# Queries by (head, 32 tokens), one sketch weight for all heads, early denominators for batch 0, and loads that wait for the weights

## The chip, the cores and the metric

The kernel runs on one core of a Trainium2 chip. A core has the engines PE (TensorE, matrix products; PEld is its loading of weights), DVE (VectorE), ACT (ScalarE), POOL (GpSimd) and SP (SyncE, which here only issues DMAs). They run beside each other and wait for each other through semaphores; 16 DMA engines move data. The metric is the device time of one launch in microseconds, the median of several runs; fewer is better.

## What is computed

Polynomial-sketch attention over 4 batches, 4 heads and 1088 tokens, and a gated feed-forward layer over the 4352 tokens that come out:

```python
def phi(x):                                   # S1, S2: (8, 32)
    a = np.einsum('rd,bhsd->bhsr', S1, x)
    b = np.einsum('rd,bhsd->bhsr', S2, x)
    return np.einsum('bhsi,bhsj->bhsij', a, b).reshape(*x.shape[:-1], 64)
q_p, k_p = phi(q), phi(k)
kv = np.einsum('bhsf,bhsd->bhfd', k_p, v)
z = np.sum(k_p, axis=2)
num = np.einsum('bhsf,bhfd->bhsd', q_p, kv)
den = np.einsum('bhsf,bhf->bhs', q_p, z)[..., None] + 1e-06
x = (num / den).transpose(0, 2, 1, 3).reshape(B * S, H * D)
out = (np.maximum(x @ w_gate, 0) * (x @ w_val)) @ w_out      # 128 -> 1536 -> 128
```

## The kernel before

Each batch has 1024 "main" tokens, 8 to a partition, and 64 "rest" tokens; the rest tokens of all batches share one tile (`kr`, `qr`, `vr`, 32 partitions for each batch).

For the keys of a batch (class `K`): `t1` transposes 32x32 blocks of k on DVE (tile `kt`), `ab` multiplies by the sketches on PE (fp32, line 251), `t2` transposes back (tile `abk`), `phi` forms the outer products (tile `kp`, line 207; for batch 0 on DVE, later on POOL), and `kvz` accumulates on PE both kv (line 278, fp16) and z (line 286, fp32), c by c, into one bank; `kvz_rest` adds the rest tokens (lines 295 and 300). `zdiag`, `w` (line 321) and `wfill` put S1 times z into the sketch weight `wst` of that batch, so that the products of the queries give the denominator too.

For the queries (class `Q`, in groups of 2 or 4 columns c of 128 tokens): `t1` (tile `qt`), `ab` with one weight for each head (line 354), `t2` (`abq`), the denominator `bw`, `dn`, `rd`, then `an`, the outer products `qp`, transposes on PE (`tr`, line 395), a copy to `pt` on ACT, `num` against `kv_bd` (line 413), and a copy to `xT` on ACT. The feed-forward layer (class `F`) goes in 102 units: `gate` and `val` on PE (lines 443, 455), `relu` on ACT (449), `prod` on DVE (tile `ht`, line 460), `out` on PE (line 469), and a store for each group. The units of the first three groups (2, 2 and 4 columns of batch 0) number 6, 6 and 12; batches 1 to 3 have two groups of 12 units each, the rest tokens one of 6.

The order on every engine is fixed when the program is built: `op` lists the steps with a duration, dependencies, an earliest time and a level, and `plan` picks one after the other. Nothing is reordered at run time: an instruction that waits holds up all behind it on its engine. `warm` puts products of zeros into gaps of PE that the plan foresees. Loads stand in the program's text: SP issues k and q of all batches one after the other, POOL the weights `wg`, `wv`, `wo` and v; `wg` waits (through `scr32`) for a part of `kr`.

Of the kernel before, what the change touches and what calls it, by code (L numbers as in the profile page):

```python
# [23 lines left out]
def kernel(  # L24
# [24 lines left out]
    GT = GC * 128  # L49
    RT = E * 128  # L50
    WARM0 = 22
# [39 lines left out]
    def load_rest(eng, dst, src):  # L91
        for b in range(B):
            eng.dma_start(
                out=dst[32 * b:32 * b + 32],
                in_=src[b, :, SM:, :].rearrange("h (t e) d -> t h (e d)", e=E),
            )

    nc.scalar.dma_start(out=s16[0:R], in_=S1[:, None, :].to_broadcast([R, 4, D]))
    nc.scalar.dma_start(out=s16[R:2 * R], in_=S2[:, None, :].to_broadcast([R, 4, D]))
    load_main(nc.sync, k_sb[0], k, 0)  # L100
    load_main(nc.gpsimd, v_sb[0], v, 0)
    load_rest(nc.scalar, kr, k)
# [29 lines left out]
    load_main(nc.gpsimd, v_sb[1], v, 1)  # L132
# [69 lines left out]
    kpr = const.tile([128, E * H, R * R], FP16, name="kpr")

    def outer(eng, dst, ab, a0, b0, n, a=None):
# [557 lines left out]
```

## Time and profile before

| what | us |
|---|---|
| time, median of 3 runs (lowest, highest) | 137.54 (137.05, 137.62) |
| the profiled execution's own time | 137.33 |
| its span, first to last instruction | 135.6 |
| busy PE, DVE, ACT, POOL | 120.6, 97.5, 77.3, 45.3 |
| DMA read from HBM, written to it | 9.05 MB, 2.23 MB |

A timeline row gives start, length, engine, line, operation, out<-in, form, count, and in brackets the idle time before it with what ended it. PE records overlap: each is longer than its distance to the next, so the pace is read from a row with a count. "PEclk" is the granted TensorE clock as a share of 2.4 GHz; 0.50 is the lower level, 1.2 GHz.

### The profile page before, as it was taken

The page shows a single profiled execution, that of the slowest core. Times are in us where ns is not written, and L with a number is a line of the kernel's source. Part 1 is how long each engine was busy: PE and PEld are TensorE (multiplying, and loading weights), DVE is VectorE, ACT ScalarE, POOL GpSimd, SP SyncE. Part 2 cuts the span into 40 slices and gives each one's busy share as a digit, 9 for nine tenths or more (in the row PEclk, how much of TensorE's full clock was granted, in tenths as well). Part 3 has the DMA queues.
Part 4 walks back from the last instruction along what each step waited for, and adds up shares of the span by engine and source line. Part 5 has one row for each costly group of instructions (what it writes and reads, how often), then busy time and mean ns, then how long its engine had stood idle before and what let it go on. Part 6 is the DMA issues. An engine that isn't in the chain of part 4 may idle for free.

```text
span 135.6 us, 2872 instructions
## 1 busy us (share of the span) xinstructions
PE 120.6 (89%) x1077; PEld 84.0 (62%) x1077; DVE 97.5 (72%) x204; ACT 77.3 (57%) x136; POOL 45.3 (33%) x64
## 2 busy tenths in 40 slices
PE   6599799359999999998989999989999999999950
PEld 6389678258885786564646774554645646656920
DVE  4359959900549758995987499679869869799950
ACT  0510004601556548689536668986985986899930
POOL 6238004998004960340189107105203403100000
PEclk9999999955599999999999999999999999999996
DMA  2989999902910010002000200010010010020011
GB/s 66 318 191 346 221 247 265 202 9 9 150 39 0 0 44 0 2 5 77 0 2 0 77 5 0 2 77 5 0 77 0 5 77 2 0 82 0 0 77 39
DMA packets 11485, 9.23 MB, mean 68 GB/s; under 512 B 3792, under 2 KB 10320, under 8 KB 11472
## 3 DMA queue, kind: packets, MB, share of 16 engines
q1 hardware_dynamic: 6864, 6.69, 16.1%
q0 software_dynamic: 3952, 2.23, 12.0%
q10 hardware_dynamic: 656, 0.14, 0.5%
q8 instruction: 8, 0.13, 0.4%
q14 instruction: 5, 0.04, 0.1%
HBM read 9.05 MB, written 2.23 MB: 83 GB/s over the span
## 4 chain that ended last, share of the span: by engine, by line
PE 58%; DMA 18%; DVE 8%; ACT 5%; POOL 4%; issue 3%; ACTq 1%; DVEq 0%; POOLq 0%
PE o_ps L469 15%; PE g_ps L443 13%; DMA wo<-in_moe_w_out_dram 13%; PE v_ps L455 13%; ACT g_sb L449 5%; DVE ht L460 4%; PE m_ps L354 4%; DMA kr<-in_k_dram 4%; PE m_ps L286 3%; PE m_ps L395 3%; PE m_ps L413 2%; DVE abq L362 2%; PE m_ps L278 2%; PE m_ps L295 2%; POOL qp L207 1%
## 5 line engine op out<-in xcount | busy, mean ns | idle before, releaser
L460 DVE TENSOR_TENSOR ht<-g_sb,v_ps 128x512 f16<-128x512 f16 x102 | 64.5, 673 | 19.0 <-ACT g_sb L449 9.6
L449 ACT ACTIVATE g_sb<-g_ps 128x512 f16<-128x512 f32 x102 | 58.0, 599 | 20.7 <-PE g_ps L443 18.1
L469 PEld LDWEIGHTS <-ht 128*128 128x128 f16 x408 | 28.5, 100 | 23.4 <-DVE ht L460 14.5
L469 PE MATMUL o_ps<-wo,ht 128*128 128x128 f16 x408 | 38.0, 224 | 4.6 <-DMA wo<-in_moe_w_out_dram 3.6
L443 PE MATMUL g_ps<-xT,wg 128*128 128x512 f16 (+1 forms) x120 | 38.8, 354 | 2.0 <-ACT g_sb L449 1.4
L455 PE MATMUL v_ps<-xT,wv 128*128 128x512 f16 (+1 forms) x120 | 39.0, 355 | 0.0
L403 ACT COPY pt<-m_ps 128x1024 f16<-128x1024 f16 (+1 forms) x10 | 8.8, 884 | 14.7 <-PE m_ps L395 14.4
L207 POOL TENSOR_TENSOR qp<-an,abq 128x1024 f16<-128x1024 f32 (+1 forms) x9 | 15.8, 1761 | 0.6
L207 POOL TENSOR_TENSOR kp<-abk 128x512 f16<-128x512 f32 x12 | 12.5, 1069 | 9.5 <-DVE abk L260 9.5
L443 PEld LDWEIGHTS <-wg 128*128 128x128 f16 x120 | 11.9, 102 | 5.9 <-issue 2.6
L368 POOL TENSOR_TENSOR bw<-abq 128x128 f32<-128x128 f32 (+1 forms) x7 | 3.0, 433 | 37.3 <-DVE abq L362 37.3
L455 PEld LDWEIGHTS <-wv 128*128 128x128 f16 x120 | 11.8, 100 | 3.5 <-issue 0.9
L354 PE MATMUL m_ps<-qt,wst 128*128 128x128 f32 (+1 forms) x80 | 10.7, 279 | 0.0
L354 PEld LDWEIGHTS m_ps<-qt,wst 128*128 128x128 f32 x80 | 9.6, 191 | 1.5 <-DVE qt L348 0.9
L423 ACT CAST xT<-m_ps 128x512 f16<-128x512 f32 (+1 forms) x10 | 5.2, 521 | 7.2 <-PE m_ps L413 6.4
L157 PE MATMUL o_ps<-zero 128*128 128x128 f16 x86 | 8.0, 262 | 1.1 <-DVE maskkv L143 1.1
L362 DVE STREAM_TRANSPOSE abq<-m_ps 128x512 f32<-128x512 f32 (+1 forms) x10 | 6.3, 631 | 2.8 <-PE m_ps L354 2.5
L157 PEld LDWEIGHTS <-zero 128*128 128x128 f16 x86 | 7.0, 122 | 1.5 <-DVE maskkv L143 1.1
L477 ACT ACTIVATE o_sb<-o_ps 128x512 f32<-128x512 f32 (+1 forms) x10 | 5.4, 538 | 4.0 <-PE o_ps L469 4.0
L286 PE MATMUL m_ps<-abk 128*128 128x64 f32 x32 | 7.4, 326 | 0.0
L251 PE MATMUL m_ps<-kt,sk 128*128 128x256 f32 (+1 forms) x16 | 6.9, 580 | 0.0
L395 PE MATMUL m_ps<-ident,qp 128*128 128x128 f16 x68 | 5.5, 219 | 0.4 <-POOL qp L207 0.4
(81 smaller groups left out, 96.7 us busy)
## 6 DMA issues: line engine op xcount, KB each, us to landing
k_sb<-in_k_dram SPq DMA_DIRECT2D x4, 512.0 KB, 4.1
q_sb<-in_q_dram SPq DMA_DIRECT2D x4, 512.0 KB, 9.2
out_dram<-o_sb SPq DMA_DIRECT2D x7, 256.0 KB, 2.0
v_sb<-in_v_dram POOLq DMA_DIRECT2D x4, 256.0 KB, 5.7
wg<-in_moe_w_gate_dram POOLq DMA_DIRECT2D x1, 384.0 KB, 7.1
wv<-in_moe_w_val_dram POOLq DMA_DIRECT2D x1, 384.0 KB, 9.6
wo<-in_moe_w_out_dram POOLq DMA_DIRECT2D x1, 384.0 KB, 17.6
out_dram<-o_sb SPq DMA_DIRECT2D x2, 128.0 KB, 2.3
```

The lines of the kernel that those rows point to most:

```text
L157: nc.tensor.matmul(ps[:, 0:128], zero, zero, start=True, stop=True)
L207: eng.tensor_tensor(out=dst.rearrange("s x (i j) -> s x i j", i=R), in0=a_src[:, :, :, None].to_broadcast([128, n, R, R]), in1=ab[:, :, No ...
L286: nc.tensor.matmul(m[:, 128:192].rearrange("f (a h j) -> f a h j", a=2, h=H), ab.rearrange("s h f -> s (h f)"), ab.rearrange("s h (a f) -> ...
L354: nc.tensor.matmul(self.ps[:, h * n * 32:(h + 1) * n * 32], wst[self.b][:, h].rearrange("p a f -> p (a f)"), self.qt[:, :, h, :], start=Tr ...
L362: nc.vector.transpose(self.absb.rearrange("p (c h) f -> p c h f", h=H), self.ps[:, 0:n * 128].rearrange("p (h c t) -> p c h t", h=H, c=n))
L395: nc.tensor.transpose(self.ps[:, p, c], self.qp[:, c * H + 2 * p:c * H + 2 * p + 2].rearrange("s h f -> s (h f)"), ident)
L403: eng.copy(out=self.pt, in_=self.ps)
L443: nc.tensor.matmul(g_ps[:, y * W:(y + 1) * W], wg[:, j], xT[:, self.col:self.col + W], start=True, stop=True)
L449: nc.scalar.activation(out=self.g_sb, in_=self.g_ps, func=ACTF.Relu)
L455: nc.tensor.matmul(self.v_ps[:, y * W:(y + 1) * W], wv[:, j], xT[:, self.col:self.col + W], start=True, stop=True)
L460: nc.vector.tensor_tensor(out=self.ht, in0=self.g_sb, in1=self.v_ps, op=ALU.mult)
L469: nc.tensor.matmul(o[:, s], self.ht[:, y * W + s * 128:y * W + (s + 1) * 128], wo[:, j], start=(j == 0 and s == 0), stop=(j == NJ - 1), sk ...
```

## The change

The queries are loaded as (head, block of 32 tokens) on partitions, 34 tokens to each, 4352 bytes in a row; the last two of the 34 are the new rest tokens of the queries, so `qr` is gone. One weight `wst[:, b]` of 128 columns holds the sketches of all four heads, and `Q.ab` is one product instead of four. `num` becomes eight products of 32 output rows (head by head) instead of two of 64. `wrest` and the filling of three `wst` tiles on POOL fall away. The store of the last group is one DMA instead of four.

For batch 0, z has its own products (`z`, `z_rest`) right behind `t2`, ahead of kv; its rest tokens come from a small load of their own (`kr0`, `vr0`); two of its four `phi` go to POOL. For every batch `kvdiag` on DVE gives way to four small `kvcopy` on ACT. S2 and the first half of k come first on SP's queue, v of batch 0 is issued by POOL behind its constants, and the loads of batches 1 to 3 are each let go by a copy on ACT that reads one element of `wv`.

```diff
-    WARM0 = 22
+    WARM0 = 34
+    def load_q(eng, b):
+        eng.dma_start(out=q_sb[b], in_=q[b].rearrange("h (t c) d -> (h t) c d", c=QC))
-    nc.scalar.dma_start(out=s16[R:2 * R], in_=S2[:, None, :].to_broadcast([R, 4, D]))
-    load_main(nc.sync, k_sb[0], k, 0)
-    load_main(nc.gpsimd, v_sb[0], v, 0)
-    load_rest(nc.scalar, kr, k)
-    load_main(nc.sync, q_sb[0], q, 0)
-    load_rest(nc.sync, vr32, v)
-    for b in range(1, B):
-        load_main(nc.sync, k_sb[b], k, b)
-        load_main(nc.sync, q_sb[b], q, b)
-    load_rest(nc.sync, qr, q)
+    nc.sync.dma_start(out=s16[R:2 * R], in_=S2[:, None, :].to_broadcast([R, 4, D]))
+    for pr in range(2):
+        nc.sync.dma_start(
+            out=k_sb[0][:, 2 * pr:2 * pr + 2],
+            in_=k[0, 2 * pr:2 * pr + 2, 0:SM, :].rearrange("h (p c) d -> p h (c d)", c=C))
+    load_rest(nc.scalar, kr0, k, [0])
+    load_q(nc.sync, 0)
...
+    nc.gpsimd.memset(kv16[:, 0], 0.0)
+    load_main(nc.gpsimd, v_sb[0], v, 0)
+    load_rest(nc.gpsimd, vr0, v, [0])
+    nc.gpsimd.memset(kv16[:, 1:], 0.0)
-    nc.gpsimd.tensor_copy(out=scr32, in_=kr[:, 0, 0:1])
+    nc.gpsimd.tensor_copy(out=scr32, in_=k_sb[0][:, H - 1, 0:1])
...
+    def load_kq(b):
+        nc.scalar.copy(out=k_sb[b][0:1, 0, 0:1], in_=wv[0:1, 0, 0:1])
+        load_main(nc.sync, k_sb[b], k, b)
+        nc.scalar.copy(out=q_sb[b][0:1, 0, 0:1], in_=wv[0:1, 0, 0:1])
+        load_q(nc.sync, b)
+        if b == 1:
+            load_rest(nc.sync, kr, k, range(B))
+            load_rest(nc.sync, vr32, v, range(B))
...
+            op("ACT", 250, load_kq, b, at=13500.0 + 3000 * (b - 1))
...
-                g = op("PE", 222, u.gate, deps=(x, *gs[-1:]))
+                g = op("PE", 222, u.gate, deps=(x, *gs[-1:]), at=10500.0)
-                v = op("PE", 222, u.val, deps=(x, *vs[-1:]))
+                v = op("PE", 222, u.val, deps=(x, *vs[-1:]), at=13500.0)
-                outs.append(op("PE", 228, u.out, deps=(p, *outs[-1:])))
+                outs.append(op("PE", 228, u.out, deps=(p, *outs[-1:]), at=16500.0))
```

What this does to the order, at three places. DVE at the head, batch 0, before (`kt` transposed k, `abk` its sketches, `kp` its features, `abr` the rest tokens' sketches, `qt` transposed q, `zd` the masked z; the row above these is the last sketch fill):

```order
L243 STREAM_TRANSPOSE kt<-k_sb_99 128x256 x4
L219 STREAM_TRANSPOSE ktr<-kr 128x256
L260 STREAM_TRANSPOSE abk<-m_ps 128x256
L207 TENSOR_TENSOR kp<-abk 128x512 x2
L227 STREAM_TRANSPOSE abr<-g_ps 128x256
L260 STREAM_TRANSPOSE abk<-m_ps 128x256
L348 STREAM_TRANSPOSE qt<-q_sb_103 128x256
L207 TENSOR_TENSOR kp<-abk 128x512 x2
L348 STREAM_TRANSPOSE qt<-q_sb_103 128x256
L348 STREAM_TRANSPOSE qt<-q_sb_103 128x512
L243 STREAM_TRANSPOSE kt<-k_sb_100 128x512
L308 TENSOR_TENSOR zd<-m_ps,maskz 128x64
```

The same place of the changed kernel:

```order
L249 STREAM_TRANSPOSE kt<-k_sb_100 128x8x64
L222 STREAM_TRANSPOSE ktr<-kr_98 32x256
L192 TENSOR_TENSOR wst<-s_t,mask 128x16x16
L267 STREAM_TRANSPOSE abk<-m_ps 128x4x64
L368 STREAM_TRANSPOSE qt<-q_sb_104 128x256
L267 STREAM_TRANSPOSE abk<-m_ps 128x4x64
L232 STREAM_TRANSPOSE abr_208<-g_ps 32x256
L205 TENSOR_TENSOR kp<-abk 128x512 x2
L368 STREAM_TRANSPOSE qt<-q_sb_104 128x256
L324 TENSOR_TENSOR zd<-m_ps,maskz 128x64
```

Two of the four `kp` and the transposes of batch 1's k no longer stand ahead of `zd`.

DVE from the third group's sketches of q (`abq`, 512 wide) to the first products `ht` of the feed-forward layer, before:

```order
L362 STREAM_TRANSPOSE abq<-m_ps 128x512
L368 TENSOR_TENSOR bw_169<-abq 128x16x8
L374 TENSOR_REDUCE dn<-bw_169 128x16
L376 RECIPROCAL rd<-dn 128x16
L381 TENSOR_TENSOR an<-abq,rd 128x128
L460 TENSOR_TENSOR ht<-g_sb,v_ps 128x512 x3
L348 STREAM_TRANSPOSE qt<-q_sb_104 128x512
```

The same place of the changed kernel:

```order
L386 STREAM_TRANSPOSE abq<-m_ps 128x512
L390 TENSOR_TENSOR bw_154<-abq 128x16x8
L396 TENSOR_REDUCE dn<-bw_154 128x16
L398 RECIPROCAL rd<-dn 128x16
L403 TENSOR_TENSOR an<-abq,rd 128x128
L249 STREAM_TRANSPOSE kt<-k_sb_101 128x8x64 x2
L475 TENSOR_TENSOR ht<-g_sb,v_ps 128x512 x3
L267 STREAM_TRANSPOSE abk<-m_ps 128x512
```

The transposes of batch 1's k, which need its load, have moved to directly ahead of the first `ht`.

ACT up to the first `relu` (line 464; `kv_140` is the kv of all batches, `pt` and `xT` as above), with what each waits for (DMASW3 is the landing of `wv`), before:

```order
L179 COPY s1rep<-g_ps 128x128 [waits PE_49]
L583 CAST vr<-vr_97 128x256 [waits DMAHW3_49,DMAHW7_49,DMAHW2_49,DMAHW1_49]
L403 COPY pt<-m_ps 128x512 [waits PE_49]
L423 CAST xT<-m_ps 128x256 [waits PE_49]
L449 ACTIVATE g_sb<-g_ps 128x512 [waits PE_49] x2
```

And in the changed kernel:

```order
L180 COPY s1rep<-g_ps 128x128 [waits PE_49]
L330 ACTIVATE kv_140<-m_ps 64x2x32 [waits PE_49,Pool_49]
L715 CAST k_sb_101<-wv 1x1 [waits DMASW3_49]
L717 CAST q_sb_105<-wv 1x1
L330 ACTIVATE kv_140<-m_ps 64x2x32 x3
L421 COPY pt<-m_ps 128x512 [waits PE_49]
L438 CAST xT<-m_ps 128x256 [waits PE_49]
L715 CAST k_sb_102<-wv 1x1
L717 CAST q_sb_106<-wv 1x1
L464 ACTIVATE g_sb<-g_ps 128x512 [waits PE_49]
```

The copies that let go the loads of batch 1 and wait for `wv` now stand ahead of the first `pt`.

## Rows read from the trace of the kernel before

**Rows 1.** The page: span, busy time, granted clock in 40 slices.
```profile
span 135.6 us, 2872 instructions
PE 120.6 (89%) x1077; PEld 84.0 (62%) x1077; DVE 97.5 (72%) x204; ACT 77.3 (57%) x136; POOL 45.3 (33%) x64
...
PEclk9999999955599999999999999999999999999996
```

**Rows 2.** What PE and POOL waited for: us in total, times, longest.
```profile
PE o_ps L469 <- DMA wo<-in_moe_w_out_dram: 3.6, 1, 3.6
...
POOL scr L129 <- DMA vr<-in_v_dram: 4.4, 1, 4.4
```

**Rows 3.** Busy time by stretch: PE, PEld, DVE, ACT, POOL, then PEclk.
```profile
25.00:28.58 3.58, 0.00 (x1) 0.10 (x2) 1.98 (x4) 1.39 (x3) 3.58 (x4) 0.83 0.86 110
28.58:37.90 9.32, 9.32 (x71) 8.14 (x71) 2.48 (x5) 2.16 (x4) 4.58 (x8) 0.52 0.49 58
37.90:120.00 82.10, 79.16 (x715) 50.32 (x712) 65.35 (x120) 59.76 (x104) 27.39 (x32) 1.00 0.06 21
```

**Rows 4.** DMA issues, us to landing (page); then the tiles k_sb and v_sb.
```profile
wv<-in_moe_w_val_dram POOLq DMA_DIRECT2D x1, 384.0 KB, 9.6
wo<-in_moe_w_out_dram POOLq DMA_DIRECT2D x1, 384.0 KB, 17.6
...
DMA to landing us min/median/max: 4.0/4.1/10.7
...
DMA to landing us min/median/max: 4.2/5.7/12.1
```

**Rows 5.** Timeline of the head, 0 to 23 us.
```profile
1.06 2.53 PE L157 MATMUL o_ps<-zero 128*128 128x128 f16 x22 [1.06 <-DVE maskkv L143]
...
6.06 1.99 PE L157 MATMUL o_ps<-zero 128*128 128x128 f16 x17
...
7.85 3.17 PE L251 MATMUL m_ps<-kt,sk 128*128 128x256 f32 x8
...
10.90 1.05 POOL L133 DMA_DIRECT2D wo<-in_moe_w_out_dram  x1
...
11.28 0.78 PE L157 MATMUL o_ps<-zero 128*128 128x128 f16 x11
...
12.62 1.72 DVE L207 TENSOR_TENSOR kp<-abk 128x512 f16<-128x512 f32 x2
...
16.74 0.27 DVE L326 TENSOR_TENSOR wst<-m_ps,maskw 128x128 f32<-128x128 f32 x1
...
18.20 0.45 DVE L362 STREAM_TRANSPOSE abq<-m_ps 128x256 f32<-128x256 f32 x1 [1.20 <-PE m_ps L354]
...
22.85 0.38 PE L443 MATMUL g_ps<-xT,wg 128*128 128x256 f16 x2
```

**Rows 6.** Timeline, PE products of the attention behind the head.
```profile
42.47 1.88 PE L251 MATMUL m_ps<-kt,sk 128*128 128x512 f32 x4
...
48.05 0.41 PE L286 MATMUL m_ps<-abk 128*128 128x64 f32 x2
```

**Rows 7.** Groups by line and form: busy us, mean ns of one, idle before.
```profile
L460 DVE TENSOR_TENSOR ht<-g_sb,v_ps 128x512 f16<-128x512 f16 x102 | 64.5, 673 | 19.0 <-ACT g_sb L449 9.6 <-PE v_ps L455 9.2 <-PE m_ps L395 0.3
...
L207 POOL TENSOR_TENSOR kp<-abk 128x512 f16<-128x512 f32 x12 | 12.5, 1069 | 9.5 <-DVE abk L260 9.5
...
L413 PE MATMUL m_ps<-pt,kv_bd 128*64 128x512 f16 x14 | 2.8, 403 | 0.0
```

**Rows 8.** Timeline of the end.
```profile
128.22 0.83 PE L469 MATMUL o_ps<-wo,ht 128*128 128x128 f16 x12
...
131.12 0.38 ACT L477 ACTIVATE o_sb<-o_ps 128x256 f32<-128x256 f32 x1 [1.21 <-PE o_ps L469]
131.53 1.74 SPq L487 DMA_DIRECT2D out_dram<-o_sb  x4
```

More of the change, by code (lines that the diff above doesn't have):

```diff
@@ L514, in plan @@
     def plan():
[L515 removed]
+        clock = dict(T0)
         taken = {n: [] for n in BUFS}
@@ L572 @@
         units += [F(*grp, i) for i in range(NJ * grp[2] // 4)]
-    T0, WGAP, WARM_UNTIL = 3400.0, 300.0, 24000.0
-    def add_rest():
-        x = Rest()
-        t1 = op("DVE", 340, x.t1, at=6400.0, level=2)
-        ab = op("PE", 450, x.ab, deps=(t1, sk_fill), level=2, bank=("g", "v"))
-        t2 = op("DVE", 340, x.t2, deps=(ab,), level=2)
-        hold("bank", ab, t2)
-        phi = op("POOL", 1100, x.phi, deps=(t2,), level=2)
-        cp = op("ACT", 400, nc.scalar.copy, at=9000.0)
-        cp.args, cp.fn = (), lambda: nc.scalar.copy(out=vr, in_=vr32)
-        return t2, phi, cp
@@ L586, in add_k, with add_rest @@
-    def add_k(b, rest, landed, gate, pieces, banks, loaded, free, behind):
+    T0 = {"PE": 4700.0, "DVE": 2900.0, "ACT": 5300.0, "POOL": 7900.0}
+    WGAP, WARM_UNTIL = 250.0, 16000.0
+    def add_rest(n, src, at, level, gate):
+        x = Rest(n, src)
+        kw = dict(level=level, gate=gate)
+        t1 = op("DVE", 360, x.t1, at=at, **kw)
+        ab = op("PE", 240, x.ab, deps=(t1, sk_fill), bank=("g", "v") if level == 2 else ("m",), **kw)
+        hold("ktr", t1, ab)
+        t2 = op("DVE", 360, x.t2, deps=(ab,), **kw)
+        hold("bank", ab, t2)
+        phi = op("POOL", 1100, x.phi, nc.gpsimd, deps=(t2,), **kw)
+        return x, t2, phi
@@ L616, in add_k @@
-        kvzs[2].bank = None
-        kvzs[2].args = (None,) + kvzs[2].args
-        hold("abk", t2s[0], kvzs[2])
-        hold("kp", t2s[0], kvzs[2])
-        zd = op("DVE", 150, kb.zdiag, deps=(kvzs[2],), **kw)
-        kv = op("DVE", 210, kb.kvdiag, deps=(kvzs[2],), **kw)
-        hold("bank", kvzs[0], kv)
-        w = op("PE", 420, kb.w, deps=(zd, s1_copy), bank=banks, **kw)
-        wf = op("DVE", 210, kb.wfill, deps=(w, *free), **kw)
+        hold("kt", t1s[0], ab)
+        for c in range(0, GC, 2):
+            for hf in range(2):
+                dve = first and hf == 0
+                phis.append(op("DVE" if dve else "POOL", 640 if dve else 1080, kb.phi, hf,
+                               nc.vector if dve else nc.gpsimd, c, 2, deps=tuple(t2s), level=1, **kw))
@@ new lines, in add_k @@
+        kr_ = op("PE", 300, kb.kv_rest, x, vt, deps=(kvs[1], rest_phi, zr), level=1, **kw)
+        hold("abk", t2s[0], z)
+        hold("kp", t2s[0], kvs[1])
+        zd = op("DVE", 200, kb.zdiag, deps=(zr, *(() if first else (kr_,))), level=lv, **kw)
+        if first:
+            hold("bank", z, zd)
+        cps = []
+        for g in range(2):
+            for r in range(2):
+                cps.append(op("ACT", 210, kb.kvcopy, g, r, deps=(kr_, *cps[-1:]), level=1, **kw))
+        hold("bank", kvs[0], cps[-1])
@@ L625, in add_k @@
+        if not first:
+            zd.deps += ()
+            hold("bank", kvs[0], cps[-1])
+            kvs[0].holds.pop()
+        w = op("PE", 420, kb.w, deps=(zd, s1_copy), bank=banks, level=lv, **kw)
+        wf = op("DVE", 200, kb.wfill, deps=(w, f0), level=lv, **kw)
         hold("bank", w, wf)
         hold("zd", zd, w)
-        wr = op("POOL", 250, kb.wrest, deps=(wf,))
-        return kv, wf, wr
+        if not first:
+            cps[-1].deps += (zd,)
+        return cps[-1], wf
     def add_q(grp, n, kv, wf, landed, gate, fast, banks):
```

365 lines of the change are left out of this document (180 added, 185 removed).

## Prediction

> **What bounds the kernel now.** I read the page first, then PE's waits, then stretches by their busy time, then the timeline of the head and of the end. The page shows PE at 89% and a granted clock that falls to half for three of the 40 slices [rows 1]; a mean hides where that is. PE's waits name it: one wait of 3.6 us, for `wo` [rows 2]. By stretches, PE does nothing from 25.00 to 28.58, and then runs at a granted clock of 0.52, the 1.2 GHz level, until 37.90 [rows 3]. `wo` was issued at 10.90 and took 17.6 us to land [rows 4, 5], beside the k and q of all batches. Behind 37.9 the clock is full and PE is busy 79.2 of 82.1 us, DVE 65.4 [rows 3]: no single wait is left there; PE and DVE take turns. So three pieces can shrink: the head until the first gate product at 22.85 [rows 5], the stretch from there to 37.9, and the end.
>
> **The pace of PE.** Twelve out products take 0.83 us with one pipeline length of 0.22 in it [rows 8], 0.056 us each, so a gate, a val or an out step costs 0.22 us at full clock. Four fp32 products of 512 columns take 1.88 [rows 6], of which 1.72 until the next may start.
>
> **The head.** 34 instead of 22 zero products, at 2.53/22 = 0.11 us each [rows 5], fill PE from 1.06 to about 4.7, when the sketches turn; S2 now has the front of SP's queue. DVE then has the sketch fill by 5.7 and the second half of `kt` by 6.4. The k products took 3.17 us for eight [rows 5] at half speed: the zero products beside them ran at 1.99/17 before and 0.78/11 behind [rows 5], after 1.6 us without work. With PE busy from 1.06 on, I take full speed, 1.72; the bounds are 1.72 and 3.17. So both `abk` are there at 8.7. z is eight fp32 products, 0.25 to 0.41 a pair [rows 6], 1.0 to 1.6 us, and the rest tokens 0.5. DVE meanwhile does two `kp` (1.72, [rows 5]) and a `qt`, so `zd` comes at about 11.0 and `wfill` ends at 12.2, against 16.74 + 0.27 = 17.0 [rows 5]. One thing stands between: PE has the first half of kv, which needs a `kp` of POOL, ahead of the q products. POOL no longer waits 4.4 us for the rest tokens [rows 2] and has no second v between `wv` and `wo`, but two memsets and two v issues more, so by estimate it issues `wo` near 7.5 (10.90 - 4.4 - 0.8 + 1.8) and then makes the rest features and two `kp` of 1.07 each [rows 7]: 9.6, 10.7, 11.8. The first fits, and costs some 0.3. The sketches of q come in one product instead of four, so `abq` can begin at 13.2; before it was 18.20, and the first gate came 4.65 later [rows 5]. The same again, plus 0.2 for the third group's products that now stand ahead of `num`, gives the first gate at 18.0: **4.8 us earlier**. On ACT the copy that waits for `wv` stands ahead of the first `pt`; `wv`, issued near 6.9 (by estimate 0.6 ahead of `wo`), lands 4.2 (a v alone) to 9.6 us later [rows 4], at 11 to 16.5. I take 12.5, as no k or q of other batches is in the queues then. `pt` needs ACT at 16.2, so this costs nothing; at 16.5 it would cost about 1.4.
>
> **From the first gate to full clock.** From 22.85 to 37.90 PE did, by its order, 7 gates, 6 vals and 6 outs (4.2 us at full clock) and about 2.4 us of kv, z and queries (1.0 of it z, at 0.25 a pair [rows 6]): 6.6 us of work in 15.05. **8.4 us were lost**, to the 3.6 wait, to the half clock behind it (9.32 x 0.48 = 4.5), and to rests. In the changed kernel the first outs come late in the order, behind 4 gates, 3 vals and batch 1's k products. `wo`, issued near 7.5, lands at 11.7 to 25.1 (4.2 to 17.6, [rows 4]); I take 17.5, between, as only `wg` and `wv` are ahead of it and the loads of batch 1 start beside it at about 15. What is late next is batch 1's k: ACT lets it go at 14.2, behind the first `kvcopy`; landing takes 4.0 to 10.7 us [rows 4], so 18.4 to 25.1. I take 18.7, near the median 4.1, since one transfer is beside it and not five. DVE stands before its transpose from about 19.2, after the three groups' denominators; all products `ht` are queued behind it. So `kt` ends at 20.5, the k products (1.72) at 22.7, and the outs of three units at 23.8. PE does 4.8 us of work from 18.0 to 23.8, so **1.0 is lost instead of 8.4: a gain of 7.4**. Against that, batch 1's k products were done ahead of the first gate before and come behind it now: **1.9 us more** (1.72 at the pace of the stretch behind). This order is also tight: batch 1's first `num` stands behind 22 of batch 0's 24 gates. POOL makes its six `kp` of 1.07 and `qp` one after the other, and DVE waits twice between `zd`, `wfill` and `abq` with no `ht` between. I count **0.5**, in bounds of 0 and 3.
>
> **The steady part.** The products of q cost the same columns. `num`: 14 products of 512 columns are 403 ns each and 2.8 us together [rows 7], half of 14 x 0.403, so the two halves of a pair run at the same time. Eight products of 32 rows and 256 columns then cost the same if four run at once (I take this), and about 0.6 us more each group if not. The Trainium skill, TensorEngine Tiling (Array Packing), Key Properties, says that tiles of any allowed width work independently, 32 too; by that nothing is added, and no run here yet shows it for 32. `kvdiag` leaves DVE; four `kvcopy` a batch come to ACT, which is busy 59.8 of 82.1 us [rows 3]. Some 0.2 us each, they can hold up a `relu`: 0 to 0.8 a batch, taken within the 0.5. **The end:** four issues of 1.74 us in all [rows 8] become one, 0.4: **1.3 saved**.
>
> **Sum.** 4.8 + 7.4 - 1.9 - 0.5 + 1.3 = 11.1 us. The profiled execution took 137.33, so 126.2; it lies 0.2 under the median shown, which I leave aside.
>
> **The rivals.**
> (a) Batch 1 starves PE: POOL's chain of `kp`, `bw`, `an`, `qp` ends after batch 0's gates are used up. For it: `num` at the 22nd of 24 gates, and every step behind a late k. Against: my count leaves some 1 us. Price 3 us of wait, and half clock behind it as after the 3.6 us wait [rows 2, 3], up to 4.5: 129 to 133.
> (b) The change doesn't do what it says: `wo` still takes 17.6 and lands at 25.1, because the let-go loads meet it. The outs wait 2.2 us, with half clock perhaps behind: 128.4 to 133. The Trainium skill, DMA: Bandwidth & Descriptors, Queues, rings and completion order, says that each DMA engine goes round the queues that have work, packet by packet; by that rule SP's loads halve the pace of what is left of `wo`. The landing of 17.6 beside them agrees.
> (c) `num` runs its 32-row products one by one: nine groups by 0.6, less what DVE covers: 130 to 131.6.
> (d) Slower than before: batch 1's k lands late and blocks DVE, all `ht` behind it. If `wv` takes its 9.6, the copies on ACT go at 16.5, k is issued at 16.8 and with 10.7 lands at 27.5: 8.3 us behind DVE's 19.2, and half clock after that, 4.5: 126.2 + 12.8 = 139. It decides from a landing of about 26 on. Against: what made 10.7 and 9.6 were each other's transfers, now apart.
>
> **How the numbers follow.** Forecast 0.70, at 126.2; (a) 0.11, (b) 0.07, (c) 0.04, (d) 0.05; 0.03 for a mix that ends within 0.5% of 137.5, which is about what a measurement of this kernel tells from no change. The forecast's own bounds: the head 1.3 faster (z at 1.0, no wait for POOL) and all of the 1.0 and 0.5 saved, with DVE's idle turns closing up by some 1: 122.6. The other way the half-speed k products (1.45), `wv` late (1.4) and 2.5 of tightness: 131.5, which also takes in most of (a), (b) and (c). Faster 0.92, same 0.03, slower 0.05.
>
> **What would show it.** The first gate near 18; `wfill` near 12; `wv` before 14, `wo` before 20 and batch 1's k before 19.5; no PE wait over 2 us and PEclk full from 8 on; the last group's store in one issue of 0.4. Wrong: a granted clock at half anywhere behind 20, a wait of DVE for `k_sb`, `num` records longer than 0.5, or PE waiting for `xT` of batch 1 between 40 and 48.

## The result, and the profile after

| what | before | after |
|---|---|---|
| time, median of 3 runs (lowest, highest) | 137.54 (137.05, 137.62) | 132.57 (131.71, 134.50) |
| the profiled execution, and its span | 137.33, 135.6 | 134.50, 132.8 |
| ratio after to before, 95% interval | | 0.962 (0.953, 0.971) |

The change makes the kernel faster by 3.8% in this comparison, in bounds of 2.9 and 4.7. The forecast was 126.2 in a range of 122.6 to 131.5: the sign holds, the time lies 6.4 above the forecast and 1.1 above the range. The profiled execution of after is the slowest of its three. Executions of one and the same program differ by up to 4.4 us here, so below a time is a median of a row of executions, and a mechanism is read from stretches of a profile.

The three executions of before in this table are long ones for that kernel. Of 27 more, run beside the experiments below, only four took 137.05 or more; their median is 135.87 (133.45 to 137.83). The seven executions of after, these three and four later ones, have a median of 133.34 (131.50 to 134.50). All of them together show a gain of some 2.5 us or 1.9%, half of what the table says. The one later comparison of the two kernels, counted from the faster executions of each alone, gives a ratio of 0.994 (0.975 to 1.013) and leaves the gain unclear.

The page of after: span, busy PE, the granted clock in 40 slices. Beside [rows 1]:

```profile
span 132.8 us, 2928 instructions
...
PE 119.1 (90%) x1104; PEld 77.6 (58%) x1104; DVE 95.3 (72%) x198; ACT 80.8 (61%) x158; POOL 47.8 (36%) x62
...
PEclk9999997799999985699999999999999999999996
```

The three slices at half clock of before ("PEclk" is the granted clock) are gone from the place where `wo` was waited for. Two weak places have come in their stead, one at slices 7 and 8, one at slices 15 to 17. PE's waits name both (us in total, times, longest); the 3.6 us for `wo` of [rows 2] are no more in this list:

```profile
PE m_ps L283 <- DMA v_sb<-in_v_dram: 2.9, 1, 2.9
PE m_ps L257 <- DVE kt L249: 2.1, 2, 1.9
```

The head, PE's timeline (start, us, engine, line, out<-in, form, count, wait), and two rows of DVE's:

```profile
5.55 1.99 PE L257 MATMUL m_ps<-kt,sk 128*128 128x256 f32 x8
...
17.43 0.38 PE L458 MATMUL g_ps<-xT,wg 128*128 128x256 f16 x2 [0.48 <-ACT xT L438]
...
21.75 3.56 PE L257 MATMUL m_ps<-kt,sk 128*128 128x512 f32 x4 [1.91 <-DVE kt L249]
```

```profile
11.21 0.19 DVE L345 TENSOR_TENSOR wst<-m_ps,maskw 128x32 f32<-128x32 f32 x1 [0.17 <-PE m_ps L340]
...
20.39 1.30 DVE L249 STREAM_TRANSPOSE kt<-k_sb 128x512 f32<-128x512 f32 x2 [1.92 <-DMA k_sb<-in_k_dram]
```

The sketch weight is filled at 11.4 (12.2 was forecast), the first gate comes at 17.43 (18.0; before 22.85, [rows 5]). Then DVE waits 1.92 for k of batch 1, which SP issued at 14.20, and all products `ht` stand behind it. That is the first weak place. The second is PE's kv of batch 2:

```profile
45.02 0.38 PE L458 MATMUL g_ps<-xT,wg 128*128 128x512 f16 x1
48.34 0.63 PE L283 MATMUL m_ps<-v_sb,kp 128*128 128x64 f16 x16 [2.95 <-DMA v_sb<-in_v_dram]
48.90 0.62 PE L432 MATMUL m_ps<-pt,kv 128*32 128x256 f16 x8
49.45 1.97 PE L308 MATMUL m_ps<-abk 128*128 128x64 f32 x8
```

It waits for v of batch 2, and POOL's timeline shows why the load is late:

```profile
41.36 1.96 POOL L205 TENSOR_TENSOR qp<-an,abq 128x1024 f16<-128x1024 f32 x1
43.60 0.45 POOL L390 TENSOR_TENSOR bw<-abq 128x128 f32<-128x128 f32 x1 [0.28 <-DVE abq L386]
43.99 0.80 POOL L90 DMA_DIRECT2D v_sb<-in_v_dram  x1
44.82 0.42 POOL L403 TENSOR_TENSOR an<-abq,rd 128x128 f32<-128x128 f32 x1
```

The issue stands behind POOL's work for the queries of batch 1, at 43.99, and the data are there 4.3 us later, at 48.30. In the trace of before the same issue came ahead of all that work, 16 us before PE's kv of batch 2 (47.92):

```profile
31.61 0.82 POOL L89 DMA_DIRECT2D v_sb<-in_v_dram  x1
```

After by stretches (length; PE, PEld, DVE, ACT, POOL; then PEclk, DMA share, GB/s), beside [rows 3]:

```profile
17.43:21.75 4.32, 2.30 (x26) 1.60 (x25) 2.29 (x7) 3.19 (x10) 1.95 (x1) 0.98 0.70 219
21.75:25.40 3.65, 3.65 (x9) 1.58 (x10) 1.77 (x4) 0.00 (x0) 0.00 (x0) 0.56 0.53 171
25.40:45.90 20.50, 19.87 (x189) 13.67 (x187) 16.86 (x33) 13.19 (x27) 14.27 (x16) 1.00 0.27 92
45.90:48.80 2.90, 0.46 (x16) 0.45 (x15) 0.51 (x1) 0.88 (x2) 2.11 (x2) 1.00 0.67 90
48.80:55.00 6.20, 6.20 (x45) 4.79 (x42) 0.68 (x2) 1.46 (x5) 0.00 (x0) 0.50 0.35 42
55.00:128.70 73.70, 71.34 (x676) 42.86 (x674) 61.19 (x111) 57.86 (x104) 17.05 (x19) 1.00 0.09 23
```

Read it as a pattern that comes twice: PE rests (4.32 us with 2.30 of work, 2.90 with 0.46), and right behind the rest it runs at 1.2 GHz (0.56 over a stretch that holds some full clock, then 0.50). Between and behind, it is busy at full clock for 97% of the time.

### The profile page after: what moved, and what is told of

Same layout as the page of the kernel before. It is cut to its first block, busy times and chain, and to the rows that moved or that the text cites. A ratio compares the mean times of both kernels' runs of the same rounds, so it can differ in the third digit from the quotient of the medians.

```text
span 132.8 us, 2928 instructions
## 1 busy us (share of the span) xinstructions
PE 119.1 (90%) x1104; PEld 77.6 (58%) x1104; DVE 95.3 (72%) x198; ACT 80.8 (61%) x158; POOL 47.8 (36%) x62
## 4 chain that ended last, share of the span: by engine, by line
PE 64%; DMA 14%; ACT 6%; DVE 6%; POOL 4%; issue 4%; POOLq 0%; DVEq 0%; ACTq 0%
PE o_ps L485 15%; PE g_ps L458 14%; PE v_ps L470 13%; DMA wv<-in_moe_w_val_dram 6%; PE m_ps L257 6%; ACT g_sb L464 5%; PE m_ps L378 5%; DMA k_sb<-in_k_dram 5%; DMA v_sb<-in_v_dram 3%; PE m_ps L308 3%; PE m_ps L415 2%; PE m_ps L432 2%; DVE abq L386 2%; DVE ht L475 2%; PE m_ps L318 2%
## 5 line engine op out<-in xcount | busy, mean ns | idle before, releaser
L464 ACT ACTIVATE g_sb<-g_ps 128x512 f16<-128x512 f32 x102 | 58.2, 599 | 15.8 <-PE g_ps L458 10.6
L458 PE MATMUL g_ps<-xT,wg 128*128 128x512 f16 (+1 forms) x120 | 37.6, 349 | 2.4 <-ACT g_sb L464 0.9
L470 PE MATMUL v_ps<-xT,wv 128*128 128x512 f16 (+1 forms) x120 | 38.1, 354 | 0.0
L485 PE MATMUL o_ps<-wo,ht 128*128 128x128 f16 x408 | 37.3, 222 | 0.5 <-DVE ht L475 0.5
L205 POOL TENSOR_TENSOR kp<-abk 128x512 f16<-128x512 f32 x14 | 14.6, 1066 | 11.3 <-DVE abk L267 6.5
L205 POOL TENSOR_TENSOR qp<-an,abq 128x1024 f16<-128x1024 f32 (+1 forms) x9 | 15.8, 1754 | 4.5 <-DVE an L403 4.1
L330 ACT ACTIVATE kv<-m_ps 64x64 f16<-64x64 f32 x16 | 3.5, 218 | 14.5 <-PE m_ps L295 7.9
L257 PE MATMUL m_ps<-kt,sk 128*128 128x512 f32 (+1 forms) x20 | 9.5, 613 | 2.1 <-DVE kt L249 2.1
L378 PE MATMUL m_ps<-qt,wst 128*128 128x512 f32 (+2 forms) x24 | 9.1, 482 | 0.0
L249 DVE STREAM_TRANSPOSE kt<-k_sb 128x512 f32<-128x512 f32 x8 | 5.4, 689 | 4.0 <-DMA k_sb<-in_k_dram 4.0
L257 PEld LDWEIGHTS m_ps<-kt,sk 128*128 128x128 f32 x20 | 4.0, 216 | 5.4 <-DVE kt L249 3.1
L283 PE MATMUL m_ps<-v_sb,kp 128*128 128x64 f16 x64 | 3.5, 193 | 3.6 <-DMA v_sb<-in_v_dram 2.9
## 6 DMA issues: line engine op xcount, KB each, us to landing
wo<-in_moe_w_out_dram POOLq DMA_DIRECT2D x1, 384.0 KB, 10.8
```

What stands on the lines that cost most here:

```text
L205: eng.tensor_tensor(out=dst.rearrange("s x (i j) -> s x i j", i=R), in0=a_src[:, :, :, None].to_broadcast([dst.shape[0], n, R, R]), in1=ab ...
L249: nc.vector.transpose(self.kt[:, :, 2 * pr:2 * pr + 2], k_sb[self.b][:, 2 * pr:2 * pr + 2].rearrange("p h (c d) -> p c h d", d=D))
L257: nc.tensor.matmul(ps[:, 0:GC * n * 32].rearrange("p (c x) -> p c x", c=GC), sk[:, hf].rearrange("p a b f -> p (a b f)"), self.kt[:, hf * ...
L378: nc.tensor.matmul(self.ps[:, i * w:(i + 1) * w], wst[:, b].rearrange("p h f -> p (h f)"), self.qt.rearrange("p x t -> p (x t)")[:, i * w: ...
L458: nc.tensor.matmul(g_ps[:, y * W:(y + 1) * W], wg[:, j], xT[:, self.col:self.col + W], start=True, stop=True)
L464: nc.scalar.activation(out=self.g_sb, in_=self.g_ps, func=ACTF.Relu)
```

## The experiments

**Theory:** two loads come late, k of batch 1 and v of batch 2; the waits for them and the half clock behind each make up what the forecast missed. **Rival (i):** the steady part is bound by the turns of PE, DVE and ACT, and a wait there is made good later. **Rival (ii):** the clock falls for another reason than PE's rest.

One table carries most of the reading: where the 9th, 17th, 25th and last of the 102 products `ht` begin (DVE, us from the start of the profiled execution), and the time of all executions.

| kernel | 9th | 17th | 25th | last | median (lowest to highest) |
|---|---|---|---|---|---|
| after | 32.13 | 43.45 | 59.22 | 127.45 | 132.57 (131.71 to 134.50) |
| after, run again (g1_after) | 30.98 | 42.30 | 58.06 | 126.28 | 133.35 (131.50 to 133.50) |
| v2 ahead of two features of batch 1 (e1_v2_early) | 31.26 | 45.05 | 54.66 | 122.89 | 128.49 (127.11 to 129.95) |
| k1 not held (e2_k1_free) | 31.00 | 42.31 | 58.02 | 126.25 | 134.03 (130.86 to 134.86) |
| both (e3_both) | 30.79 | 44.58 | 54.19 | 122.42 | 129.27 (128.85 to 129.48) |
| zero products at both waits (e4_zeros) | 30.76 | 42.07 | 54.64 | 122.87 | 130.48 (129.73 to 132.19) |
| v2 behind batch 1's features (f1_v2_rest) | 30.07 | 41.38 | 50.99 | 119.22 | 126.33 (126.22 to 126.83) |
| the same, k1 not held (f2_v2_k1) | 29.97 | 41.28 | 50.89 | 119.12 | 126.69 (124.98 to 127.39) |
| f1 without the hold (g3_rest_no_hold) | 32.02 | 43.23 | 52.84 | 121.07 | 128.05 (126.89 to 128.56) |
| f1, last store in four issues (g2_end4) | 31.35 | 42.66 | 52.27 | 120.50 | 128.00 (126.24 to 128.25) |
| f1, 22 zero products at the start (g4_warm22) | 29.63 | 40.95 | 50.55 | 118.79 | 126.37 (125.85 to 126.66) |
| after without the hold (f3_no_hold) | 32.38 | 43.59 | 57.83 | 126.06 | 134.37 (133.12 to 136.15) |
| after, z behind kv (f4_z_behind) | 33.84 | 44.78 | 61.79 | 130.01 | 136.40 (134.56 to 137.07) |

From the 25th on all of them take the same 68.2 us. From the 17th to the 25th they take 9.6 where v of batch 2 is early, 12.57 with zero products in the wait for it, and 14.24, 15.7 to 15.8 or 17.01 where it is late. These last three go with 3.41, 6.83 and 10.24 us of half clock behind the wait.

### v of batch 2 early, first try

```diff
-            outer(eng, self.kp, self.absb, 0, R, E * H)
+            outer(eng, self.kp, self.absb, 0, R, E * H); load_main(nc.gpsimd, v_sb[2], v, 2) if self.n == 128 else None
...
-            lv = (op("POOL", 900, load_main, nc.gpsimd, v_sb[b], v, b, gate=[0, -1, 10, 20][b],
+            lv = (op("POOL", 900, lambda *a: load_main(*a) if a[1] is not v_sb[2] else None, nc.gpsimd, v_sb[b], v, b, gate=[0, -1, 10, 20][b],
```

> The changed kernel, but the load of v of batch 2 is issued by POOL some 15 us earlier, behind the features of the shared rest tile (about 28 us) instead of behind POOL's chain of batch 1 (43.99); nothing else moves. Theory (two late loads, v2 and k1, and the half clock behind each make up what the prediction missed): the wait of 2.95 us before PE's kv of batch 2 goes, and with it the half clock from 48.85 to 55.67 (6.83 us at half, so 3.4): 132.6 - 6.3 = 126 to 128, with k1's wait still there. Rival (i), the steady part is bound by the order in which PE, DVE and ACT take turns, and a wait there is made good later: within 1 us of 132.6. Rival (ii), the clock does not fall because of the wait: the wait goes, the half clock stays: 129.5 to 130.

Measured 128.49, 4.1 under after and half a microsecond above the theory's bounds. The wait for v and the half clock behind it are gone: 9.61 instead of 15.77 us from the 17th to the 25th product. But from the 9th to the 17th it takes 13.79 instead of 11.32. POOL's timeline of this run, PE's waits for POOL in total and the one of them that is not in the head, and the stretch behind:

```profile
28.32 0.80 POOL L90 DMA_DIRECT2D v_sb<-in_v_dram  x1
29.15 2.10 POOL L205 TENSOR_TENSOR kp<-abk 128x512 f16<-128x512 f32 x2
```

```profile
PE m_ps L283 <- POOL kp L205: 1.2, 2, 0.7
...
31.30 0.35 PE L283 MATMUL m_ps<-v_sb,kp 128*128 128x64 f16 x6 [0.73 <-POOL kp L205]
```

```profile
33.80:37.30 3.50, 3.50 (x13) 1.97 (x12) 0.81 (x2) 0.67 (x4) 0.08 (x1) 0.51 0.04 13
```

The issue costs POOL 0.8 us, and two features that batch 1's kv waits for stand behind it. PE rests 0.73 for them (the other 0.5 of the 1.2 is in the head, at 14.19, and the other kernels have it too), and 3.41 us of half clock follow from 33.86, 2.6 us behind that rest: 0.73 + 3.41/2 = 2.4, the 2.5 that the stretch has grown by. So the load was the cause, and the new place is a cause of the same kind, smaller. Rival (i) has fallen.

### k of batch 1 not held

```diff
-    load_q(nc.sync, 0)
+    load_q(nc.sync, 0); load_main(nc.sync, k_sb[1], k, 1)
...
-        nc.scalar.copy(out=k_sb[b][0:1, 0, 0:1], in_=wv[0:1, 0, 0:1])
-        load_main(nc.sync, k_sb[b], k, b)
+        nc.scalar.copy(out=k_sb[b][0:1, 0, 0:1], in_=wv[0:1, 0, 0:1]) if b > 1 else None
+        load_main(nc.sync, k_sb[b], k, b) if b > 1 else None
```

> The changed kernel, but k of batch 1 is issued by SP right behind q of batch 0 and not held until wv has landed; q of batch 1 and all later loads stay held. Theory: k1 is there before 18, so DVE's wait of 1.9 us for it and the half clock from 21.54 to 24.95 (3.41 us, 1.7 lost) go; the weights, which now have one more transfer beside them, land about 1 to 1.5 us later, which gives back up to 1: 129 to 131, with the wait for v of batch 2 and the half clock behind it unchanged. Rival (i): within 1 us of 132.6. Rival (iii), the hold of k1 is what lets the weights land in time: wv or wo come so late that PE waits for them, 133 or more.

Measured 134.03: a miss for the theory. PE's k products of batch 1 hardly wait any more (0.2), and still begin no earlier than in after (21.75):

```profile
19.87 0.38 PE L458 MATMUL g_ps<-xT,wg 128*128 128x256 f16 x2 [0.48 <-ACT xT L438]
...
22.19 1.98 PE L257 MATMUL m_ps<-kt,sk 128*128 128x512 f32 x4
```

The first gate came at 19.87 in this execution, 2.4 later than in the profile of after. The same happens in other kernels with the same head (e1_v2_early: 19.87), where the k products of batch 0 take 3.7 us instead of 1.99 because the granted clock is full only from about 10. So the late k of batch 1 and such a late head run beside each other: whichever ends last counts, and the wait for k shows only where the head was early. Rival (iii) named this time but not its cause, weights too late: `wo` landed at 18.24 and nobody waited for it. The profiled executions of this kernel and of g1_after, 133.32 and 133.34, are level.

### Both edits

The two diffs above together.

> The edits of both runs before together: v of batch 2 early and k of batch 1 not held. Theory: both gains add, 132.6 - 6.3 - 2.6 = 123.7, in bounds of 123 to 126; no stretch of half clock behind the head. Rival (i): 131 or more, the two waits were cover for something else. If v2 early takes bandwidth from q1 and the rest tokens, a new wait between 30 and 45 shows it.

Measured 129.27, a miss as well, and for the reasons just given: 13.79 us from the 9th to the 17th again (POOL's delay), and no gain from k.

### Both waits filled with zero products

```diff
+            for _ in range(34 if self.b == 1 else 0):
+                nc.tensor.matmul(ps[:, 0:128], zero, zero, start=True, stop=True)
...
+                for _ in range(50 if self.b == 2 else 0):
+                    nc.tensor.matmul(self.m[:, 256:384], zero, zero, start=True, stop=True)
```

> The changed kernel with zero products put on PE ahead of the two places where it waits: 34 ahead of batch 1's k products, 50 ahead of batch 2's kv. Both loads are as late as before; PE only does not rest while they come. Theory: the two waits stay (5 us of them), the two half-clock stretches go (10.2 us at half, 5.1 lost), less some 1 to 2 us where the zero products run on past the landing: 128.5 to 130. Rival (ii), the clock falls for another reason than PE's rest: the half clock stays where it was and the time is 132.5 to 134.

Measured 130.48, half a microsecond above the theory's bounds; it tells the clock from the wait. Page and PE's timeline:

```profile
PEclk9999999999999999999999999999999999999998
```

```profile
43.85 2.96 PE L282 MATMUL m_ps<-zero 128*128 128x128 f16 x50
46.87 0.63 PE L287 MATMUL m_ps<-v_sb,kp 128*128 128x64 f16 x16
```

The load is as late as ever (issued at 42.62, landed at 46.83), PE only does something meanwhile (the zero products end at 46.81, just as the data land), and the clock does not fall. The mean granted clock is 0.982 to 0.999 in the four executions, against 0.954 to 0.971 in the seven of after. From the 17th to the 25th product it takes 12.57: 15.77 - 12.57 = **3.20 us were the half clock**, and 12.57 - 9.61 = **2.96 were the wait itself**. Rival (ii) has fallen; for the first place that rests on little, as the clock didn't fall there in g1_after either.

### v of batch 2 behind batch 1's features

```diff
             outer(eng, self.kp[:, hf, sl], self.absb[:, sl], hf * 16, hf * 16 + R, n * H)
+            if (self.b, hf, lo) == (1, 1, 2):
+                load_main(nc.gpsimd, v_sb[2], v, 2)
```

(and the same change of `lv` as in the first try)

> The changed kernel, v of batch 2 issued by POOL behind the last features of batch 1's k (about 31.3), where POOL rests 4.8 us in the changed kernel's trace; nothing else moves. The first try put it ahead of two of these features, and PE then waited for POOL there (1.2 us) and fell to half clock from 33.86. Theory (the load was late, and its place in POOL's order is what matters): it lands near 36, no wait of PE for v or for POOL's features over 0.5 us, no half clock behind 25: the time between the 17th and the 25th product ht falls from 15.77 to 9.6 us as in the first try, and the stretch from the 9th to the 17th stays at 11.3 instead of 13.8: 132.6 - 6.2 = 126.4, in bounds of 125.5 to 128. Rival (the half clock between 33 and 37 of the first try had another cause than POOL's delay): the stretch from the 9th to the 17th takes 13 or more again and the time is that of the first try, 128.5.

Measured **126.33** (126.22 to 126.83), ratio to before 0.943 (0.938 to 0.949): as the theory said to 0.1 us. POOL's timeline, PE's, and the stretches:

```profile
27.15 2.10 POOL L205 TENSOR_TENSOR kp<-abk 128x512 f16<-128x512 f32 x2
29.18 0.80 POOL L90 DMA_DIRECT2D v_sb<-in_v_dram  x1
34.08 2.08 POOL L205 TENSOR_TENSOR kp<-abk 128x512 f16<-128x512 f32 x2 [4.09 <-DVE wst L347]
```

```profile
42.95 0.38 PE L460 MATMUL g_ps<-xT,wg 128*128 128x512 f16 x1
43.17 0.63 PE L285 MATMUL m_ps<-v_sb,kp 128*128 128x64 f16 x16
43.78 0.40 PE L434 MATMUL m_ps<-pt,kv 128*32 128x256 f16 x8
```

```profile
21.26:25.00 3.74, 3.74 (x30) 2.58 (x31) 3.35 (x6) 1.22 (x3) 0.92 (x1) 1.00 0.40 132
25.00:45.00 20.00, 19.87 (x198) 13.67 (x195) 15.79 (x30) 13.14 (x28) 14.57 (x16) 1.00 0.40 114
45.00:120.40 75.40, 73.10 (x700) 44.38 (x699) 61.88 (x112) 58.86 (x109) 17.91 (x21) 1.00 0.12 26
```

Now the issue stands where POOL rests 4.09 us anyway, the data land at 34.46, and kv follows its gate without a wait. One row of POOL moved by 15 us is worth about 6 us, as much as the distance between the forecast and the result.

### The same, with k of batch 1 not held

> As the run with v of batch 2 behind batch 1's features, and k of batch 1 issued at the start by SP, not held. Theory: where the head runs at full clock early (first gate near 17.4), the wait of 1.9 us for k of batch 1 goes; where it does not (first gate near 19.9), there is no such wait to gain: 0 to 2 us under the run beside it, 124.5 to 127.5. Rival (not holding k1 delays v of batch 0 and the weights, as in the first try, where v of batch 0 landed at 12.2): 0.5 to 2 us above the run beside it.

Measured 126.69 beside 126.33: no gain that these times can show. It doesn't decide between the two sides, though. In the profile PE has no wait for k of batch 1, but the granted clock is at half from 12.13 to 15.54 and the first gate comes at 18.96 instead of 17.51. Of the five profiles with k of batch 1 issued early (this one, e2, e3, f3 and g3) none has the head at full clock throughout, so what the early load gains beside an early head stays open. (The lowest execution, 124.98, is the fastest seen of any kernel; it has no trace.)

### No hold at all

SP's program has all k, q and rest tokens in a row behind those of batch 0; ACT's copies that read `wv` are gone. In the trace of f3_no_hold k of batch 1 is issued at 2.73, of batches 2 and 3 at 14.45 and 19.07.

```diff
     load_q(nc.sync, 0)
+    for b in range(1, B):
+        load_main(nc.sync, k_sb[b], k, b)
+        load_q(nc.sync, b)
+        if b == 1:
+            load_rest(nc.sync, kr, k, range(B))
+            load_rest(nc.sync, vr32, v, range(B))
...
```

First on the changed kernel as it is:

> The changed kernel without the hold: SP issues k and q of batches 1 to 3 and the rest tokens at the start, as the kernel before does, and ACT's copies that wait for wv are gone. Theory of the prediction (the hold is what brings the weights in time): wg, wv and wo land 4 to 8 us later (wo at 22 to 25 instead of 17.2), the first gate waits for wg, PE rests and a stretch of half clock follows: 135 to 139. Rival (the weights are early because POOL issues them at 5.3 to 6.4 instead of 10.9, and the hold adds nothing): wo lands by 19 and the time is 130 to 132, since k of batch 1 is then early.

Measured 134.37, 1.0 to 1.8 above after: neither side's number. The landing (KB, us) and PE's first outs:

```profile
wo<-in_moe_w_out_dram POOLq DMA_DIRECT2D x1, 384.0 KB, 18.9
```

```profile
24.01 0.61 PE L421 MATMUL m_ps<-ident,qp 128*128 128x128 f16 x8
25.32 0.83 PE L491 MATMUL o_ps<-wo,ht 128*128 128x128 f16 x12 [0.70 <-DMA wo<-in_moe_w_out_dram]
```

Without the hold `wo` takes 18.9 us, longer than before the change (17.6), but it is issued at 6.42 instead of 10.90 and so lands at 25.3 instead of 28.5. PE waits 0.70 for it where it waited 3.6 [rows 2]. Then on the kernel with v of batch 2 in its place:

> The kernel with v of batch 2 issued behind batch 1's features, but without the hold: k and q of batches 1 to 3 and the rest tokens are issued by SP at the start. Theory (the hold lets the weights land early, and the order, in which the outs now come late, already hides a late wo): wo at about 25 again, a wait of under 1 us for it, the first gate 1 to 3 us later by wg at 15.5 and v of batch 0 at 12.8: 127 to 129. Rival (the hold is what removed the stall): PE rests for 2 us or more and a stretch of half clock follows: 130 or more. Rival (the hold costs what it brings, since it makes k of batch 1 late): 126 or less.

Measured 128.05, as the theory said: `wo` at 25.44, a wait of 0.98, no half clock. By the medians the hold is worth 128.05 - 126.33 = 1.7 us, in the head (9th product at 32.02 instead of 30.07). But this profile has a late head, with full clock only from 9.65; against the late heads that have the hold (9th product at 31.26 in e1_v2_early and 31.35 in g2_end4) it loses 0.7. So the hold is worth 0.7 to 1.7 us.

The long stall of before is short even without the hold, for two reasons. POOL issues `wo` 4.5 us earlier, and it lands 3.1 to 3.2 earlier. And the outs now stand behind the k products of batch 1, so PE asks for `wo` at 24.5 to 24.6, about as late as before (25.00), although the first gate comes 3 us earlier. No run takes the two apart.

### Denominators of batch 0 behind its kv again

```diff
-            z = op("PE", 1300, kb.z, deps=tuple(t2s), level=lv, bank=banks, **kw)
+            z = op("PE", 1300, kb.z, deps=tuple(kvs), level=lv, bank=banks, **kw)
```

> The changed kernel with the denominators of batch 0 behind its k features again (z only once kv of batch 0 is done); the planner then moves the query steps of batch 0 behind it and fills PE with zero products. Theory of the prediction (z ahead is a part of the 4.8 us of the head): wfill ends 2 to 4 us later, the first gate comes at 20 to 21.5 instead of 17.43; since k of batch 1 lands at about 20 to 21 all the same, part of it is given back: 133 to 136. Rival (the head is bound by the weights or by k of batch 1): the first 16 products ht come no later than in the changed kernel, and the time is 131.5 to 133.

Measured 136.40, 3 to 4 above after and 0.4 above the theory's bounds. DVE's `wfill` and the first gate:

```profile
14.80 0.23 DVE L324 TENSOR_TENSOR zd<-m_ps,maskz 128x64 f32<-128x64 f32 x1 [4.03 <-PE m_ps L295]
15.81 0.19 DVE L345 TENSOR_TENSOR wst<-g_ps,maskw 128x32 f32<-128x32 f32 x1 [0.79 <-PE g_ps L340]
```

```profile
20.94 0.38 PE L458 MATMUL g_ps<-xT,wg 128*128 128x256 f16 x2 [0.47 <-ACT xT L438]
```

The weight is filled 4.6 later and the first gate comes 3.5 later than in the profile of after. This part of the change carries most of the head's gain, 3.5 of 5.4, as forecast. Not all of it reaches the end: the wait for k of batch 1 goes, and the 9th product comes 1.7 later, the 17th 1.3. Another 1.2 is lost up to the 25th, where the half clock behind the wait for v lasts 10.24 us instead of 6.83.

### Three more parts

The changed kernel again, beside the runs below and g3_rest_no_hold:

> The changed kernel again, on the chip and beside the runs of the three that follow. Theory (two late loads and the half clock behind the second): 130 to 133, some 5 to 6 us above the kernel with v of batch 2 issued behind batch 1's features (126.3).

133.35, just above the bounds. In its profile the wait of 1.9 for k of batch 1 is there again, but no half clock follows it; the wait of 2.8 for v and half clock for 6.8 us behind it are there as before, 15.76 us from the 17th to the 25th product.

The last group's store in four issues, on the kernel with v of batch 2 in its place:

```diff
-                nc.sync.dma_start(
-                    out=blocks[:, QC - E:].rearrange("b s t m -> b t s m"),
-                    in_=o_sb[:, 0:n])
+                for b in range(B):
+                    nc.sync.dma_start(
+                        out=blocks[b, QC - E:].rearrange("s t m -> t s m"),
+                        in_=o_sb[32 * b:32 * b + 32, 0:n])
```

> The kernel with v of batch 2 issued behind batch 1's features, but the last group's store in four issues, one a batch, as before the change. By the prediction's count the single issue saves 1.3 us: 127.6. Rival (by the traces of the two kernels, where the last copy to o_sb begins 4.5 us ahead of the end before and 4.2 behind the change: the landing of one store is as long as the three issues it saves): 126.3 to 126.8, and 4.4 to 4.6 us from the last copy's start to the end.

The median of 128.00 looks like the prediction's count, but the profile shows that 1.28 of it lies ahead of the first product `ht` (22.41 instead of 21.13, a late head). From the last copy's start to the end of the span it is 126.5 - 121.68 = 4.8 us with four issues and 124.6 - 120.40 = 4.2 with one:

```profile
122.08 1.76 SPq L504 DMA_DIRECT2D out_dram<-o_sb  x4
```

The 4.8 is above the rival's 4.4 to 4.6 too. The single issue saves 0.6, not 1.3.

22 zero products at the start instead of 34 (`WARM0`), on the same kernel:

> The kernel with v of batch 2 issued behind batch 1's features, with 22 zero products at the start instead of 34, as before the change. Theory (PE's rest between the zero products and the sketches keeps the granted clock at half until about 10): k products of batch 0 at half speed, first gate near 19.9 instead of 17.4, of which 1.3 is given back since the wait for k of batch 1 goes: 126.8 to 128.5. Rival (the zero products change nothing, the clock in the head differs from run to run anyway): 126.3, within 0.5.

126.37: nothing lost. In its profile the clock is full from 7.59, the k products of batch 0 take 3.06 and the first gate comes at 18.34, 0.8 later than in the run with 34, and the wait of 1.3 for k of batch 1 disappears in turn.

## Why the prediction was wrong, point by point

**The step that failed is "tightness".** The prediction put what the new order may cost beyond its listed steps at 0.5, in bounds of 0 and 3, and looked for it in POOL's features, DVE's turns and the first `num` of batch 1. It followed POOL's compute steps past their new places, but not the DMA issue that stands among them: v of batch 2, with PE's kv of batch 2 behind it. That load costs 2.96 of wait and 3.20 of half clock, **6.2 us**; with it moved the kernel runs at 126.33, where the forecast said 126.2. Rival (a), "batch 1 starves PE", given a chance of 0.11, had the right price (3 us of wait and up to 4.5 of half clock) and, with 129 to 133, the right time; but it put the cause into the chain of batch 1, and what PE waits for is the next batch's load behind that chain. The range ended at 131.5 and took in only most of this rival. (Its lower end adds up to 126.2 - 1.3 - 1.0 - 0.5 - 1 = 122.4, not 122.6.) Two of the prediction's signs of being wrong came: a clock at half behind 20, and DVE's wait for `k_sb`.

**The other steps, against the kernel with the load in its place** (f1_v2_rest):

| term of the sum | forecast | measured |
|---|---|---|
| first gate earlier | 4.8 | 22.85 - 17.51 = 5.3, where the head is early; 3.0 where it is late (19.87) |
| from the first gate to the last copy, shorter | 7.4 - 1.9 - 0.5 = 5.0 | (131.12 - 22.85) - (120.40 - 17.51) = 5.4 |
| the end | 1.3 | (135.6 - 131.12) - (124.6 - 120.40) = 0.3; 0.6 by the run with four issues |
| sum | 11.1 | 11.0 (span 135.6 to 124.6) |

That the sum comes out to 0.1 us is in part luck. The profile of before, from which the forecast counts, is one of that kernel's long executions, with full clock only from 10.31; the profile of f1_v2_rest has it from 4.38. By the medians of executions run beside each other f1_v2_rest gains 135.85 - 126.33 = 9.5 us, 1.6 less than forecast. Some 1.2 of the head's gain in the table is this clock (k products 3.17 before, 1.99 here). The forecast put it down to the 34 zero products; with the same 34 the clock is full by 5.3 in six profiles and only from 9.5 or later in six. The terms between the first gate and the last copy are measured only as a sum.

- **The head** was right in mechanism, and the run with z behind kv shows its price. The two bounds for the k products of batch 0, 1.72 and 3.17, were not a choice to make: 1.99 and 3.7, above the upper bound, are both there, in executions of the same head.
- **The stall behind the first gate.** That it would go was right; `wo` at 17.5 (measured 17.17) was the reason given. Even at 25.3 it costs only 0.7 to 1 us of wait, because PE asks for it at 24.5. The prediction had this in its own count (outs at 23.8) and in rival (b), whose 2.2 us of wait measured 0.7 to 1.0, with no half clock behind it in g3_rest_no_hold.
- **k of batch 1** was taken to land at 18.7 and landed at 20.3. In the profile of after this cost 1.9 of wait and half clock for 3.41 us; in g1_after the wait alone. Issued early, it gained nothing in two trials, both with half clock in the head of their profiles. Rival (d) did not come.
- **`num`** by 32 rows runs four at a time: eight products in 0.40 (x8 row at 43.78 in f1_v2_rest) where two of 64 rows took 0.4. Rival (c) has fallen, and the Trainium skill, TensorEngine Tiling (Array Packing), Key Properties, agrees.
- **The end** was mis-sized: three issues of 0.44 are saved, but the span ends 3.4 us behind the one store's issue (f1_v2_rest) and 2.7 behind the last of four (g2_end4).

The Trainium skill, DMA: Bandwidth & Descriptors, Queues, rings and completion order, says that a DMA engine goes round the queues that have work; the trace agrees in direction: `wo` takes 10.8 us with the hold and 18.9 without. The same page, Anatomy of one DMA, fits a transfer issued by GpSimd as 2.0 us and its bytes at 436 GB/s; for the 256 KB of v that gives an estimate of 2.6. The trace has 4.3, and the measurement decides.

## What to carry to other kernels

When a change moves work on an engine that also issues loads, list the loads among the moved rows and ask of each who stands behind its landing; a load's issue belongs into a rest of its engine, behind the steps that others wait for and ahead of the long chain that they don't. A wait of PE costs more than its length where half clock follows it: here 2.95 us cost 6.2, and 0.73 us cost 2.5. Before paying for an early landing, see when its first reader comes in the new order: the hold of the loads gave 0.7 to 1.7 us, and without it the wait for `wo` was 1 us at most. And before crediting a gain to a change, see how far executions of the kernel before lie apart: here by 4.4 us, more than the change gained.

## What the runs showed of the hardware that was not expected

- A rest of PE is followed by half clock in some executions and not in others of the same program: behind the wait of 1.9 us the clock was at half for 3.41 us in one profile of after and full in the other. Behind the wait of 2.8 to 2.95 for v of batch 2 it fell in all five profiles that have this wait and no zero products in it: for 6.8 us in after, g1_after and e2_k1_free, 10.2 in f4_z_behind, 3.4 in f3_no_hold.
- The rest ahead of a fall can be short. In e1_v2_early and e3_both PE rested 0.73 and 0.74 us, and 3.41 us of half clock followed. In f2_v2_k1 the clock fell at 12.13 behind a rest of 0.52, where f1_v2_rest had a rest of 0.57 at the same place and kept its clock. Why one falls and the other not stays open.
- In the same way the granted clock is full from 4.4 or only from about 10 in executions with the same head, which moves the first gate by 2.4 us. More or fewer zero products at the start made no difference that the times show (126.33 with 34, 126.37 with 22).
- The outer product on 32 partitions took POOL 2.01 us (`kpr` of batch 0), where the same on 128 partitions takes 1.06; POOL's spans are rough, and what else was in it wasn't tried.
